# Turning q, the exponentials and the normalised rows by DMA instead of on TensorE in batches 2 to 4

## The chip, the cores and the metric

One core of one Trainium2 chip runs the whole program. The metric is the time of one execution on the device in microseconds (us); the median of several runs counts. The engines are TensorE (PE, with its weight loads as PEld), VectorE (DVE), ScalarE (ACT), GpSimd (POOL) and SyncE (SP). POOL and SP issue the transfers.

## The reference

Four batches, eight heads, 768 tokens, head size 64. Per head an 8x8 matrix P is normalised five times over rows and columns (Sinkhorn) and mixes the eight blocks of 96 keys and values. Each block of 96 queries then attends to its own mixed block of 96 keys. The result, 768 x 512 per batch, goes through a two-dimensional Fourier transform (the real part is added to it), a layer normalisation and an MLP of 512 to 2048 to 512.

```python
k_sorted = np.einsum('bhij,bhjcd->bhicd', P, k_b)
v_sorted = np.einsum('bhij,bhjcd->bhicd', P, v_b)
scores = scale * np.matmul(q_b, k_sb.transpose(0, 1, 2, 4, 3))
attn = np.exp(scores - np.max(scores, axis=-1, keepdims=True))
attn = attn / (np.sum(attn, axis=-1, keepdims=True) + 1e-09)
x = np.matmul(attn, v_sb)                  # heads side by side: 768 x 512
u = x + np.real(np.fft.fft(np.fft.fft(x, axis=1), axis=2))
un = (u - mu) / np.sqrt(var + 1e-06)
out = u + np.maximum(un @ w_ch1, 0.0) @ w_ch2
```

## The kernel before

Work is cut into steps, and a planner (`Plan`) orders them once, when the program is built. Each step has for each engine that may run it a cost in nanoseconds; a transfer has also a size (`kb`, in a model of DMA bandwidth) or a landing time (`hop`). The planner walks through a modelled time, gives each engine the step that could start first, and among steps within 40 ns the one of highest priority: earlier batches first, MLP products (`prio` from 1e6) last, so that they fill what attention leaves free on PE. Buffers come from rings of a few tiles (`ring`), the eight PSUM banks among them. The order that results is fixed; on the chip each engine takes its instructions in that order and waits on semaphores. SP's and POOL's queues of transfers are ordered in the same way.

One batch goes through these stages.

- *Loads.* `load_kq` (L408, POOL) loads k and q of a pair of heads as float16 with six tokens on one partition; `load_v` (L400, SP) loads v as float32.
- *Mix.* `q_mix`: PE turns q of a pair in twelve transposes (L592), and an ACT or DVE copy (L381 or L385) makes qT, 128 x 768. `k_mix`: PE multiplies k by the matrix of P (L609), and two copies (L383 or L387) write kz, which has the keys of a head on 64 of 128 partitions. `v_mix` (L563, L565) and `v_move` (L575, twelve transfers a batch) make vs, the mixed values with the key position on partitions.
- *Attention,* in halves of four blocks. `maxima`: four products qT by kz (L661) put queries on partitions, and DVE takes the row maxima (L664). `scores`: four products (L676) write minus the maximum into a bank, broadcast along the keys' partitions, and four more (L680) add kz by qT, so that the scores stand transposed, keys on partitions; one ACT exponential follows (L685). `minus_one` (L695 ACT or L697 DVE) subtracts 1 and writes eT. `values`: four products of eT by vs (L708), where row 96 of eT is all ones, then DVE's reciprocal and product (L713, L714) into xr.
- *Post.* Folding and the DFT over the sequence (L752, L764), the DFT over the model size (L797, L801), the residual (L828, L830), sums on POOL (L845, L846), a store of u to DRAM (L852, SP), statistics (L863), normalisation (L880), and `transpose_u`: four PE transposes of each tile of rows (L896) and a copy to unT.
- *MLP,* in two groups a batch: 64 products L924, ReLU on ACT (L930), 48 products L945, the sum with u (L952), which is loaded again by SP (L910), and an indirect store by POOL (L967).

Attention of the next batch runs beside post and MLP of those before it. Rings that matter here: `sm` (4 tiles of exponentials), `mxs` (6), eT (3, one a head), banks (8), unT (2).

Of the kernel before, what the change touches and what calls it, by code (L numbers as in the profile page):

```python
# [9 lines left out]
F32 = mybir.dt.float32  # L10
F16 = mybir.dt.float16
# [16 lines left out]
XSC = 64.0  # L28
RSC = 1.0 / XSC

PERM = np.array([6 * (p % 16) + p // 16 for p in range(BLK)])

# [270 lines left out]
def kernel(  # L305
# [60 lines left out]
    ring("mh", 1, [128, 2, 2 * LT], F16)  # L366
    plan.rings["eT"] = Ring([const.tile([97, NB, BLK], F16, name=f"eT{i}") for i in range(3)])
    eTs = plan.rings["eT"].tiles
# [35 lines left out]
    def load_kq(b, hp, need):  # L404
        hs = slice(2 * hp, 2 * hp + 2)
        for d, src, tag in ((k16, k, "k16"), (q16, q, "q16")):
            d[b, hp] = Buf(tag)
            step("load_" + tag, b, {"G": 740}, lambda e, t=d[b, hp], src=src: nc.gpsimd.dma_start(  # L408
                t.t, src[b, hs].rearrange("h (p g) d -> p h (g d)", g=G)),
                w=[d[b, hp]], kb=393, need=need)  # L410

# [38 lines left out]
    selj = const.tile([64, 128], F32, name="selj_sb")  # L450
    junk = const.tile([128, DM], F16, name="junk")
    nc.vector.memset(junk, 1.0)
# [36 lines left out]
    rsel = const.tile([BLK + 3, 2, BLK + 1], F16, name="rsel_sb")  # L489
    lm = const.tile([128, 2, 2, 385], F16, name="lm_sb")  # L490

# [91 lines left out]
    def q_mix(b, hp):  # L583
        qT[b, hp] = Buf("qT")
        pQ = Buf("bank")

# [8 lines left out]
        def ev(e):  # L595
            copy(e, qT[b, hp].t.rearrange("x (i g c) -> x i g c", g=G, c=16),
                 bank(pQ, [128, G, 128], F16).rearrange("x g (i c) -> x i g c", c=16))
        plan.chain(("psQ", b, {"T": 530}, f, [q16[b, hp]], [pQ]),
                   ("qT", b, {"A": 799, "V": 545}, ev, [pQ], [qT[b, hp]]))

    def k_mix(b, hp, gh):
# [11 lines left out]
        def ev(e, hh):  # L613
            r = slice(64 * hh, 64 * hh + 64)
            dst = kzs[hp][r, hh].rearrange("x (i g c) -> x i g c", g=G, c=16)
            copy(e, dst[:, :, 3 * gh:3 * gh + 3, :],
                 bank(pK, [128, 3, 128])[r].rearrange("x g (c i) -> x i g c", c=16), SCALE)
        plan.chain(("psK", b, {"T": 360}, f, [k16[b, hp], (kron[b], hp // 2)], [pK]),
# [48 lines left out]
    def scores(n, half):  # L667
# [5 lines left out]
        def f(e):  # L673
# [4 lines left out]
            for j in range(4):  # L678
# [7 lines left out]
                sms[n, half].t, bank(pS, [BLK, 4, BLK]), AF.Exp), [pS], [sms[n, half]]))  # L686

    def minus_one(n, half):
        if half == 0:
# [10 lines left out]
    def values(n, half):  # L700
# [3 lines left out]
        def f(e):  # L704
            ps = bank(pN, [BLK, 4, D + 1])
            for j in range(4):
                i = 4 * half + j
                nc.tensor.matmul(ps[:, j, :], eT[n].t[:, i, :],  # L708
                                 vs[2 * (b % 2) + h // 4][:, i, (D + 1) * (h % 4):(D + 1) * (h % 4 + 1)])
# [175 lines left out]
    def transpose_u(b, i, m):  # L885
# [3 lines left out]
        if (b, t // 4) not in unT:  # L889
            unT[b, t // 4] = Buf("unT")  # L890
        pY = Buf("bank")

# [130 lines left out]
    for hp in range(4):  # L1023
# [6 lines left out]
    warm(banks[7], 2)  # L1030
    ptm = plan.rings["sm"].tiles[3].rearrange("p a c -> p (a c)")[0:64, 0:256].rearrange(
        "p (i n) -> p i n", n=32)
# [63 lines left out]
    for b in range(B):  # L1096
# [63 lines left out]
```

## Time and profile before

| | |
|---|---|
| median of three runs | 347.85 us (345.82 to 349.72) |
| profiled execution | 349.94 us, span 348.2 us |
| PE busy | 316.3 us (91%) |
| DVE, ACT, POOL busy | 222.1, 212.3, 136.9 us |
| mean granted PE clock | 0.969 |
| DMA | 41.28 MB, 119 GB/s; q0 26.0% and q1 24.7% of 16 engines |
| chain that ended last, by engine | PE 62%, DVE 13%, issue 7%, DMA 7%, POOL 5%, ACT 4% |
| attention's products L676, L680, L661, L708 | 23.1, 22.9, 20.1, 19.5 us busy, 256 each |
| MLP's products L924, L945 | 89.0 us (512), 89.5 us (384) |

Matmuls overlap, and a busy time counts each of them from start to modelled end; what a run of matmuls really takes is read from the pace at which they start, in the timeline or the chain. The chain follows, from the last instruction backwards, what released each step. A stretch of the run is best judged by the busy times in that stretch, as the share over the whole span mixes stages of different kinds.

### The profile page before, as it was taken

The page shows a single profiled execution, that of the slowest core. Times are in us where ns is not written, and L with a number is a line of the kernel's source. Part 1 is how long each engine was busy: PE and PEld are TensorE (multiplying, and loading weights), DVE is VectorE, ACT ScalarE, POOL GpSimd, SP SyncE. Part 2 cuts the span into 40 slices and gives each one's busy share as a digit, 9 for nine tenths or more (in the row PEclk, how much of TensorE's full clock was granted, in tenths as well). Part 3 has the DMA queues.
Part 4 walks back from the last instruction along what each step waited for, and adds up shares of the span by engine and source line. Part 5 has one row for each costly group of instructions (what it writes and reads, how often), then busy time and mean ns, then how long its engine had stood idle before and what let it go on. Part 6 is the DMA issues. An engine that isn't in the chain of part 4 may idle for free.

```text
span 348.2 us, 8075 instructions
## 1 busy us (share of the span) xinstructions
PE 316.3 (91%) x3042; PEld 206.4 (59%) x3042; DVE 222.1 (64%) x577; ACT 212.3 (61%) x474; POOL 136.9 (39%) x190
## 2 busy tenths in 40 slices
PE   0998987867998999999989999999999999999994
PEld 0368854755766655678747867656556455554541
DVE  6688995996787799399989989983550602101001
ACT  5598885885787455788986846617537354260620
POOL 8879340175460599932100116651351420112111
PEclk9998998995799999999999999999999999999999
DMA  7999959079669397793530122243070330403212
GB/s 180 217 255 263 143 93 197 10 157 194 165 145 144 85 262 218 119 140 72 91 64 2 63 62 71 84 152 105 25 217 34 107 119 2 151 32 99 81 47 76
DMA packets 34799, 41.28 MB, mean 119 GB/s; under 512 B 4465, under 2 KB 26448, under 8 KB 34760
## 3 DMA queue, kind: packets, MB, share of 16 engines
q0 software_dynamic: 14992, 16.97, 26.0%
q1 hardware_dynamic: 19768, 23.80, 24.7%
q8 instruction: 24, 0.39, 0.5%
q14 instruction: 15, 0.12, 0.1%
HBM read 35.36 MB, written 12.58 MB: 138 GB/s over the span
## 4 chain that ended last, share of the span: by engine, by line
PE 62%; DVE 13%; issue 7%; DMA 7%; POOL 5%; ACT 4%; SPq 1%; POOLq 0%; DVEq 0%; ACTq 0%
PE bank L924 21%; PE bank L945 20%; DMA u_dram<-u 3%; DMA xr<-xr 3%; PE bank L676 3%; PE bank L680 2%; PE bank L708 2%; ACT kz L383 2%; PE bank L511 2%; DVE xr L714 2%; DVE mxs L664 2%; PE bank L592 1%; PE bank L661 1%; PE bank L801 1%; PE bank L752 1%
## 5 line engine op out<-in xcount | busy, mean ns | idle before, releaser
L930 ACT ACTIVATE hr<-bank 128x384 f16<-128x384 f32 x128 | 62.2, 490 | 59.3 <-PE bank L924 58.8
L945 PE MATMUL bank<-w2sb,hr 128*128 128x512 f16 x384 | 89.5, 379 | 0.0
L924 PE MATMUL bank<-unT,w1sb 128*128 128x384 f16 x512 | 89.0, 329 | 0.3 <-DVE unT L385 0.3
L924 PEld LDWEIGHTS <-w1sb 128*128 128x128 f16 x512 | 49.6, 99 | 32.5 <-issue 1.1
L967 POOL DMA_INDIRECT out_dram<-outt,idx_sb x23 | 22.7, 988 | 101.5 <-DVE outt L952 48.6
L945 PEld LDWEIGHTS <-hr 128*128 128x128 f16 x384 | 36.1, 98 | 37.9
L952 DVE SCALAR_TENSOR_TENSOR outt<-ur,bank 128x512 f32<-128x512 f32 x24 | 16.4, 683 | 49.1 <-PE bank L945 49.1
L880 DVE TENSOR_SCALAR un<-u,mv,rstd 96x512 f16<-96x512 f32 (+1 forms) x32 | 21.5, 703 | 33.4 <-PE bank L896 32.5
L685 ACT ACTIVATE sm<-bank 96x384 f32<-96x384 f32 x64 | 28.6, 484 | 8.3 <-PE bank L680 5.0
L664 DVE TENSOR_REDUCE mxs<-bank 96x4 f16<-96x384 f32 x64 | 31.6, 542 | 0.3
L714 DVE TENSOR_TENSOR xr<-bank,rz 96x256 f16<-96x256 f32 x64 | 26.9, 421 | 2.2
L845 POOL TENSOR_TENSOR u<-u,P 96x257 f32<-96x257 f32 (+1 forms) x16 | 11.9, 743 | 35.9 <-ACT u L381 21.5
L676 PE MATMUL bank<-nident_sb,mxs 96*96 96x96 f16 x256 | 23.1, 215 | 3.1 <-ACT u L381 2.0
L863 DVE BATCH_NORM_STATS2 st<-u 96x6 f32<-96x512 f32 (+1 forms) x32 | 21.8, 680 | 1.9 <-POOL u L846 1.9
L661 PE MATMUL bank<-kz,qT 128*96 128x96 f16 x256 | 20.1, 212 | 3.1 <-ACT kz L383 1.8
L680 PE MATMUL bank<-qT,kz 128*96 128x96 f16 x256 | 22.9, 214 | 0.0
L695 ACT ACTIVATE eT<-sm 96x384 f16<-96x384 f32 x46 | 22.7, 520 | 0.3 <-PE bank L708 0.2
L383 ACT ACTIVATE kz<-bank 64x384 f16<-64x384 f32 x45 | 21.3, 485 | 1.8 <-DVE kz L387 1.3
L676 PEld LDWEIGHTS <-mxs 96*96 96x96 f16 x256 | 18.9, 130 | 5.4 <-issue 2.9
L381 ACT COPY u<-bank 96x512 f32<-96x512 f32 (+1 forms) x26 | 14.5, 582 | 11.2 <-PE bank L830 4.5
L427 POOL TENSOR_TENSOR v<-v 128x384 f32<-128x384 f32 x11 | 11.7, 1066 | 22.6 <-ACT v L381 17.9
L708 PE MATMUL bank<-vs,eT 97*96 97x65 f16 x256 | 19.5, 213 | 0.9 <-DVE kz L387 0.4
(119 smaller groups left out, 549.7 us busy)
## 6 DMA issues: line engine op xcount, KB each, us to landing
u_dram<-u SPq DMA_DIRECT2D x32, 192.0 KB
ur<-u_dram SPq DMA_DIRECT2D x24, 256.0 KB
v<-in_v_dram SPq DMA_DIRECT2D x11, 384.0 KB
k<-in_k_dram POOLq DMA_DIRECT2D x16, 192.0 KB, 4.6
q<-in_q_dram POOLq DMA_DIRECT2D x16, 192.0 KB, 5.8
vs<-vo SPq DMA_DIRECT2D x42, 65.0 KB
w1sb<-in_moe_w_ch_dram POOLq DMA_DIRECT2D x4, 512.0 KB, 10.7
w2sb<-in_moe_w_ch_dram POOLq DMA_DIRECT2D x4, 512.0 KB, 8.2
```

Of the source, the lines that this page charges most:

```text
L383: nc.scalar.activation(dst, src, AF.Copy, scale=scale)
L661: nc.tensor.matmul(ps[:, j, :], qT[b, hp].t[:, col], kzs[hp][:, hh, col])
L664: ("max", b, {"V": 548}, lambda e: nc.vector.tensor_reduce(mxs[n, half].t, bank(pS, [BLK, 4, BLK]), axis=AX.X, op=ALU.max), [pS], [mxs[n, ...
L676: nc.tensor.matmul(ps[:, j, :], mxs[n, half].t[:, j:j + 1].broadcast_to([BLK, BLK]), nident, start=(j == 0), stop=False, skip_group_check= ...
L680: nc.tensor.matmul(ps[:, j, :], kzs[hp][:, hh, col], qT[b, hp].t[:, col], start=False, stop=True, skip_group_check=True)
L685: ("exp", b, {"A": 487}, lambda e: nc.scalar.activation(sms[n, half].t, bank(pS, [BLK, 4, BLK]), AF.Exp), [pS], [sms[n, half]]))
L695: nc.scalar.add(dst, sms[n, half].t, -1.0)
L708: nc.tensor.matmul(ps[:, j, :], eT[n].t[:, i, :], vs[2 * (b % 2) + h // 4][:, i, (D + 1) * (h % 4):(D + 1) * (h % 4 + 1)])
L714: nc.vector.tensor_tensor(xr2[b % 2][0:BLK, 4 * half:4 * half + 4, D * h:D * (h + 1)], ps[:, :, 0:D], rz.t[:, :, None].broadcast_to([BLK, ...
L924: nc.tensor.matmul(ps, w1sb[:, mc, 128 * fc:128 * fc + 128], unT[b, gr].t[:, mc, :], start=(mc == 0), stop=(mc == 3))
L930: nc.scalar.activation(dst, bank(pH, [128, 384]), AF.Relu)
L945: nc.tensor.matmul(ps, hr[f4].t[:, fc % 4, 128 * t:128 * (t + 1)], w2sb[:, fc, :], start=(fc == 0), stop=(fc == 15))
```

## The change

In the first batch nothing changes but the order of the queries in a block, which becomes the natural one (`PERM`, with the tables made from it), and ring sizes. In the second to fourth batch:

- q is loaded with another layout, token g*128+p on partition p, in two transfers a pair (rows of 64 elements, for six times 64 before). SP issues a DMA transpose of the q tile, which writes qT; the PE transposes and the copy go.
- kz gets the opposite sign. Scores are multiplied once a half, queries on partitions; DVE takes the minimum (of the negated scores) from that bank, and ACT makes the exponential from the same bank with the minimum as its bias: four activations of 96x96 a half, as each block has a bias of its own, for one of 96x384.
- The subtraction of 1 writes a float16 tile es, padded to 128 columns a block with ones (set once), and SP issues a DMA transpose of es into the half of eT that `values` reads. The ones arrive in rows 96 to 127.
- Of the eight tiles of normalised rows of a batch, seven are turned by DMA transposes issued by SP; the eighth, of 97 rows, stays on PE.
- The planner gets costs for these: 1200 ns of SP for each turn and 2500 ns until it has landed, 1080 ns for the four exponentials, 1600 ns of POOL and a size of 600 in the place of 393 for a q load.
- To make room, `sm` has three tiles for four, `mxs` four for six (first batch only), rings `mns` and `es` have three each, eT has 128 partitions for 97, and the tile for warming up PE shares memory with a table.

```diff
+QKB = 600
-PERM = np.array([6 * (p % 16) + p // 16 for p in range(BLK)])
+PERM = np.arange(BLK)
...
-    ring("mxs", 6, [BLK, 4], F16)
-    ring("sm", 4, [BLK, 4, BLK], F32)
+    ring("mxs", 4, [BLK, 4], F16)
+    ring("mns", 3, [BLK, 4], F32)
+    ring("es", 3, [BLK, 4, 128], F16)
+    ring("sm", 3, [BLK, 4, BLK], F32)
...
+                tq = t.t.rearrange("p a x -> p (a x)").rearrange("p (g h d) -> p g h d", g=G, h=2)
+                for hh in range(2):
+                    nc.gpsimd.dma_start(tq[:, :, hh], src[b, 2 * hp + hh].rearrange(
+                        "(g p) d -> p g d", g=G))
+            step("load_" + tag, b, {"G": 740 if b == 0 or tag == "k16" else 1600}, f,
+                 w=[d[b, hp]], kb=393 if b == 0 or tag == "k16" else QKB, need=need)
...
     def q_mix(b, hp):
         qT[b, hp] = Buf("qT")
+        if b:
+            step("turn_q", b, {"S": 1200}, lambda e: nc.sync.dma_start(
+                qT[b, hp].t.rearrange("x (g p) -> x g p", g=G),
+                q16[b, hp].t.rearrange("p a x -> p (a x)"), transpose=True),
+                r=[q16[b, hp]], w=[qT[b, hp]], hop=2500)
+            return
...
+    def turned(n, half):
...
+        def f(e):
+            ps = bank(pS, [BLK, 4, BLK])
+            for j in range(4):
+                col = slice(BLK * (4 * half + j), BLK * (4 * half + j + 1))
+                nc.tensor.matmul(ps[:, j, :], qT[b, hp].t[:, col], kzs[hp][:, hh, col])
+        def x(e):
+            for j in range(4):
+                nc.scalar.activation(sm.t[:, j, :], bank(pS, [BLK, 4, BLK])[:, j, :], AF.Exp,
+                                     bias=mn.t[:, j:j + 1], scale=-1.0)
...
+        plan.chain(
+            ("psS", b, {"T": 185}, f, [qT[b, hp]] + [("kz", hp, hh, g_) for g_ in range(2)], [pS]),
+            ("max", b, {"V": 548}, lambda e: nc.vector.tensor_reduce(
+                mn.t, bank(pS, [BLK, 4, BLK]), axis=AX.X, op=ALU.min), [pS], [mn]),
+            ("exp", b, {"A": 1080}, x, [pS, mn], [sm]))
+        step("minus", b, {"V": 459, "A": 518}, g, r=[sm], w=[es])
+        step("turn_e", b, {"S": 1200}, lambda e: nc.sync.dma_start(
+            et.t[:, 4 * half:4 * half + 4, :], es.t.rearrange("q j k -> q (j k)"), transpose=True),
+            r=[es], w=[(et, half)], hop=2500)
...
+        if b and (i, m) != (0, 1):
+            step("turn_u", b, {"S": 1200}, lambda e: nc.sync.dma_start(
+                unT[b, t // 4].t[:, :, BLK * (t % 4):BLK * (t % 4) + BLK],
+                un[b, i, m].t[0:BLK], transpose=True),
+                r=[un[b, i, m]], w=[(unT[b, t // 4], t % 4)], hop=2500)
+            return
...
+    for t in plan.rings["es"].tiles:
+        nc.gpsimd.memset(t[:, :, BLK:128], 1.0)
...
             for half in range(2):
+                if b:
+                    turned(n, half)
+                    continue
                 maxima(n, half)
                 scores(n, half)
                 minus_one(n, half)
```

More of the change, by code (lines that the diff above doesn't have):

```diff
@@ L366 @@
     ring("mh", 1, [128, 2, 2 * LT], F16)
-    plan.rings["eT"] = Ring([const.tile([97, NB, BLK], F16, name=f"eT{i}") for i in range(3)])
+    plan.rings["eT"] = Ring([const.tile([128, NB, BLK], F16, name=f"eT{i}") for i in range(3)])
     eTs = plan.rings["eT"].tiles
@@ L595, in ev @@
         def ev(e):
-            copy(e, qT[b, hp].t.rearrange("x (i g c) -> x i g c", g=G, c=16),
-                 bank(pQ, [128, G, 128], F16).rearrange("x g (i c) -> x i g c", c=16))
+            copy(e, qT[b, hp].t.rearrange("x (p g) -> x p g", g=G),
+                 bank(pQ, [128, G, 128], F16).rearrange("x g p -> x p g"))
         plan.chain(("psQ", b, {"T": 530}, f, [q16[b, hp]], [pQ]),
```

28 lines of the change are left out of this document (20 added, 8 removed).

## Prediction

> **What bounds the kernel now.** I read the slices of the page first, then the busy times by stretch, the chain that ended last, the groups of instructions by shape, and last the timeline and the DMA landings where the change cuts in.
>
> Busy times by stretch (us from:to, length, then busy time and count of each engine, granted clock, DMA share, GB/s):
>
> ```profile
> 60.00:80.00 20.00, 16.24 (x268) 14.07 (x269) 18.39 (x44) 16.67 (x39) 7.99 (x12) 0.93 0.48 92
> 80.00:100.00 20.00, 17.42 (x156) 12.87 (x155) 14.15 (x44) 13.69 (x34) 9.87 (x15) 0.72 0.79 185
> ...
> 160.00:180.00 20.00, 18.42 (x264) 13.62 (x263) 17.67 (x58) 18.33 (x43) 2.46 (x3) 1.00 0.47 96
> 180.00:200.00 20.00, 19.08 (x302) 15.56 (x300) 18.59 (x53) 15.26 (x37) 1.02 (x1) 1.00 0.09 29
> 200.00:220.00 20.00, 20.00 (x163) 13.34 (x162) 17.94 (x55) 11.03 (x27) 6.70 (x9) 1.00 0.23 68
> 220.00:240.00 20.00, 19.95 (x138) 11.88 (x136) 16.52 (x37) 9.77 (x26) 12.26 (x15) 1.00 0.46 138
> ```
>
> From 200 us PE is full. Up to 100 us no single engine is: PE, DVE and ACT take turns. The chain in its last third is PE alone, the two MLP products:
>
> ```profile
> 258.22 10.40 PE bank L924 x64
> 268.62 0.86 PE bank L945 x4
> 269.48 0.35 PE bank L896 x8
> ...
> 280.11 10.40 PE bank L924 x64
> ```
>
> So a group of the MLP costs 10.4 us for 64 L924 and 12 x 0.86 us for 48 L945, 20.8 us; eight groups are 166. The first L924 starts at 86.2 us. From there PE always has MLP work to take while attention waits, provided the written order puts it there; from there to the end of the products PE idles some 7 us (1.8 to 100 us, 5.0 from 100 to 200). PE time removed after 86 us is therefore time saved, PE time removed before it is not.
>
> **The change part by part.** Pace is read where PE runs without a gap, since a busy mean (215 ns for L676) counts overlap.
>
> ```profile
> 162.45 0.26 PEld L676 LDWEIGHTS <-mxs 96*96 96x96 f16 x4
> 162.63 0.26 PEld L680 LDWEIGHTS <-kz 128*96 128x96 f16 x4
> 162.81 0.30 PEld L676 LDWEIGHTS <-mxs 96*96 96x96 f16 x4
> ```
>
> In the chain, twelve q transposes in a row:
>
> ```profile
> 168.89 0.46 PE bank L592 x12
> ```
>
> *Second score product (L676, L680) gone in 48 halves:* 0.36 us from one half to the next (162.45 to 162.81), 17.3 us. *q transposes (L592) gone for 12 pairs:* twelve a pair in 0.46 us, 5.5 us. *Transposes of normalised rows (L896) gone for 21 of 32 tiles:* eight in 0.34 to 0.35 us, 0.17 a tile, 3.6 us. Together 26.4 us of PE. Before 86 us lie 12 of batch 1's 16 halves (48 of its 64 L676 stand in 60 to 80 us) and its four q pairs: 4.3 + 1.8 = 6.1 us, counted as nothing. That leaves **20.3 us** saved.
>
> *ACT.* One exponential of 96x384 (484 ns) becomes four of 96x96. Between 204 ns for 96x2 (L874) and 484 ns for 96x384 lie 0.73 ns an element, so 273 ns each, 1.09 us a half, 0.61 more; 48 halves add 29 us. The row with a bias (L873, 293 ns for 96x2) would make it 362 ns each and 46 us. Copies saved: about nine qT (804 ns) and 14 unT (477 ns), 14 us. ACT goes from 212 to 227 us (ends 212 and 245), below PE either way. The cover is MLP on PE; without it, 0.6 us a half over 48 halves, 29 us, would be exposed. I take 0. DVE loses a few copies and keeps its maximum at 542 ns; 0.
>
> *The turn of the exponentials: a new wait.* PE's L708 now waits for SP's issue and a transfer. The planner reserves 1.2 us for issue plus 2.5 us, 3.7. Behind a late L708 stand all later products, MLP too, as PE takes them in order. The trace has no such transfer. The nearest are SBUF to SBUF:
>
> ```profile
> 174.67 0.55 SPq L553
> ...
> 175.26 2.45 DMA xr<-xr
> ...
> DMA to landing us min/median/max: 4.5/5.0/5.8
> ```
>
> The first is at a DMA share of 0.47: 3.04 us from issue. The last line is vs<-vo from POOL near 22 us, when DMA is saturated. The ends are 3.04 and 5.8 us. Three es tiles let three halves be in flight, so PE loses an excess once per three halves. In batch 1, during loads of weights and u (share 0.5 to 0.8), I take 5.0: 1.3 too late; the first six halves are hidden because L708 of that batch waits for vs anyway, which leaves ten halves, 3.3 rounds, **4.3 us**. In batches 2 and 3 the share was 0.09 to 0.47 for most of the time, the 3.04 us row is nearest: nothing late in 10.7 rounds. The built order also covers: between the first and last L708 of batches 2 and 3 PE's queue holds 128 L924 and 96 L945 (41 us), where the kernel before had 0 and 40.
>
> A rule of the Trainium skill speaks against this part: VectorE: DVE Perf Modes, section The three transpose paths and its rules, prefers TensorE for a 128x128 transpose when PSUM will do and gives 1309 ns to the crossbar against 390. The measured TensorE pace here, 0.46 us for twelve 128x64, is far below its 390 ns. By the Trainium skill's crossbar figure a half (three such squares) would take 3.9 us and, on top of issue, be about 1.4 us late in every round, an estimated 20 us, which would leave no gain. No transfer in this trace shows it.
>
> *SP and its queue.* 81 turns of 1.2 us are 97 us of SP in about 250. They stand in one queue with u stores, ur loads and v loads; in the built order batch 2's four v loads come behind 16 turns of batch 1. SP already waits in ur loads, which would then hold a turn back:
>
> ```profile
> SPq L910 <- DVE outt L952: 76.9, 16, 14.1
> SPq L852 <- POOL u L846: 59.1, 25, 14.4
> ```
>
> Most of these lie in the last third, with no exponential behind them; 0, with the first rival as the other end.
>
> *q loads.* Twelve loads become two issues each: 12 x 0.74 = 8.9 us of POOL. Rows shrink from 1536 to 256 bytes, 1536 rows for 256. At equal time a byte nothing is added; at equal time a row (97 ns: 26% of 16 x 348 us over 14992 packets) 80 rows an engine add 7.7 us a load. POOL carries the chain around 89 to 117 us. I take **2.0 us** (ends 0 and 31, the four loads of batch 1). *u turns* replace L896 and a copy; in the built order three MLP groups (62 us) stand behind the last post; 0. *First batch:* three memsets before POOL's loads (0.32 us for twice the size) and a smaller sm ring: **1.0 us** (ends 0 and 3).
>
> Sum: -20.3 + 4.3 + 2.0 + 1.0 = -13.0 us. The profiled execution took 349.94 (span 348.2 and 1.7 around it), 2.1 above the median 347.85 of the three runs. On the median: **335 us**.
>
> **Rivals.**
>
> *Turns late everywhere (slower).* Place: L708 of all three batches, 14 exposed rounds. It decides where 14 rounds eat 20.3 - 3.0 = 17.3 us: 1.24 late each, landing 4.9 us after issue. At the 5.8 us end: 14 x 2.1 = 29 us, -20.3 + 3.0 + 29.4 = +12.1, **360 us**. For it: 5.0 us landings of vs<-vo, stores of 192 KB of 3.70 and 8.10 us at 72 and 76 us, 12 times the bytes of the 2.45 us row. At 8.10 + 1.2 us it would be 409. Against: DMA was little used from 160 us on.
>
> *Turns follow one another in one stream (slower, far).* Units of 96 KB: 48 e, 21 u, 12 q of two, 93. From about 60 us to 285 us (last post must leave three groups) they fit if one takes under 2.4 us. At half the 8.10 us store, 4.05 each: 60 + 93 x 4.05 + 41.6 = about **478 us**. Half the 3.70 us store, 1.85, fits. The Trainium skill's 1309 ns a square (VectorE: DVE Perf Modes) would be 3.9 us a unit, were squares not to overlap; its DMA: Bandwidth & Descriptors, Latency and other measured facts, has 261 GB/s for transposes instead, 0.4 us a unit.
>
> *The gain is eaten (no change).* DVE and ACT bind batches 1 to 3 rather than PE: at 160 to 200 us they are 36.3 and 33.6 of 40 us busy beside PE's 37.5; ACT's net 14 us then come back as PE idle, beside the 7.3 us of the other terms: -20.3 + 21.3 = +1.0, **349 us**. Against: the built order gives PE 41 us of MLP there.
>
> *PE's own idle shrinks too.* More MLP among the attention also fills the 7 us idle after 86 us, and no added term shows: 347.85 - 20.3 - 7 = **321 us**.
>
> **How the numbers follow.** Forecast 335 us: 0.42, own range 325 to 344. 321 us: 0.10. Eaten, 349 us: 0.10. Late turns, 352 to 409 with 360 as its price: 0.32, nearly all over 1%. One stream, 478: 0.06. 1% either way is about what a measurement of this kernel can tell from no change. Faster 0.52, same 0.10, slower 0.38. The range reaches from 318 to 378 us: it leaves out the stream rival, a tenth for the tail of late turns, and little below.
>
> **What would show it.** Right: L676 down to 64 and L592 to 48; PE busy about 290 us; PE in front of L708 waiting for eT's transfer under 10 us in all; turns landing 3 to 4 us after issue from 140 us on; the last attention interleaved with L924. Wrong: tens of us of PE idle ended by the transfer of eT or qT, SP busy in the turns well over 1.2 us each, or first L924 much later than 86 us, which would put the fault in the first batch or the loads. A full PE and still no gain would refute the pace of the removed products.

## The result and the profile after

The changed kernel takes 358.36 us (median of 4 runs, 355.94 to 359.55) against 348.11 us (345.82 to 349.72) for the kernel before in the same session: ratio 1.0291, interval 1.0209 to 1.0373. It is 2.9% slower; the forecast was 335 us. The profiled execution took 359.55 us, its span is 357.8 us and the mean granted TensorE clock 0.916.

First the busy times by stretch of the changed kernel, the same stretches and columns as shown of the kernel before, and then its total busy times from the page:

```profile
60.00:80.00 20.00, 10.54 (x96) 6.98 (x95) 17.91 (x43) 12.41 (x44) 6.49 (x9) 0.89 0.54 101
80.00:100.00 20.00, 8.79 (x70) 6.89 (x70) 11.15 (x23) 7.27 (x26) 9.38 (x13) 0.50 0.98 180
...
160.00:180.00 20.00, 15.92 (x129) 8.96 (x125) 12.84 (x28) 13.43 (x48) 11.32 (x15) 0.95 1.30 175
180.00:200.00 20.00, 16.61 (x160) 11.74 (x160) 13.49 (x47) 14.24 (x41) 1.38 (x2) 0.79 0.68 148
200.00:220.00 20.00, 19.29 (x164) 11.51 (x165) 18.49 (x43) 15.38 (x50) 10.15 (x13) 1.00 0.79 145
220.00:240.00 20.00, 16.31 (x164) 11.86 (x162) 16.44 (x42) 12.93 (x40) 6.47 (x9) 0.99 0.53 134
```

```profile
PE 297.7 (83%) x2430; PEld 185.1 (52%) x2430; DVE 238.3 (67%) x606; ACT 205.7 (57%) x556; POOL 148.3 (41%) x204
```

PE lost the work that it was to lose: 612 fewer instructions, and 18.6 us less busy time (316.3 before). That is less than the 26.4 us of the prediction; the largest part of the rest is in the 512 MLP products L980 (L924 before), which are busy for 96.3 us in place of 89.0, some of them at a lower granted clock (0.50 from 104 to 108 us, 0.79 in the mean from 180 to 200). But span minus busy time, PE's idle time, went from 31.9 to 60.1 us, 28.2 more. The difference, 9.6 us, is the longer span. The idle time grew in every part of the attention: by 14.3 us from 60 to 100 us (19.33 of 40 us busy, 33.66 before), by 8.2 us from 100 to 200, by 4.4 us from 200 to 260. DVE, which was to lose a few copies, has 16.2 us more to do.

The chain in order of time in the changed kernel shows the worst of the waits (start, length, what):

```profile
82.00 1.46 PE bank L758 x16
...
85.21 9.59 DMA eT<-es
94.80 0.02 issue
94.83 0.35 DVE es L727
95.18 0.10 DVE rz L763
...
95.31 0.43 DVE xr L764
...
95.78 0.48 PE bank L952 x4
...
105.21 0.71 PE bank L980 x3
105.92 7.14 DMA eT<-es
...
113.14 0.04 ACT es L725
...
160.10 1.03 ACT sm L719 x4
...
161.78 4.82 DMA eT<-es
...
259.50 3.45 DMA eT<-es
...
289.95 10.07 PE bank L980 x62
```

A turn issued at 85.21 us is released 9.59 us later; one at 161.78 us after 4.82, and one at 259.50 us, right behind a load of u, after 3.45. These are landings on the chain. By the packets and semaphores of the trace the mean is 5.0 us for the 16 turns of the second batch and 3.2 us for 28 of the 32 later ones (the semaphore records of the other four are not complete), and a turn with nothing ahead of it takes 2.3. What waits for the first is not PE in front of the value product, as the prediction had it, but DVE, which cannot write the next `es` tile until the turn has read it. All that stands behind on DVE (L763, L764, a copy) comes 6.9 us late, and PE starts its transposes of the first batch's normalised rows (L952), which wait for L764, only at 95.78. The first MLP product starts at 105.0 us (86.2 before). At the end of the run the price of an MLP product is what it was, 10.07 us for 62 where 64 took 10.40, and the four exponentials of a half follow one another in 1.03 us. The landing is only the last part of the time for which that `es` tile is held. Two lines of SP's queue in the second batch, with no turn between them (start, length):

```profile
74.11 1.29 SPq L734 DMA_TRANSPOSE eT<-es  x1
...
85.21 3.15 SPq L734 DMA_TRANSPOSE eT<-es  x2
```

The turn at 85.21 us is the seventh of its batch, and its `es` tile had been written by 71.1 us (the seventh writing in the trace), 14.1 us before the issue. eT has three tiles of two halves, so six turns find a free one; the seventh needs the tile of the first head, which the value product L758 reads only at 82.00 us, in the first line of the chain above. In the next two batches the tile of the seventh turn lies for 13.3 and 9.2 us in the same way, and the turn is issued within 2 us of the first L758 of its batch (182.4 and 229.1 us).

The waits of the changed kernel, all engines (total us, times, longest):

```profile
POOL q L417 <- DMA qT<-q: 36.0, 2, 19.2
...
ACT sm L719 <- DVE mns L730: 12.6, 10, 3.4
...
ACT es L725 <- DMA eT<-es: 11.5, 7, 3.1
...
DVE es L727 <- DMA eT<-es: 7.4, 2, 6.9
PEld L758 <- DMA vs<-vo: 7.4, 2, 5.6
...
PE bank L952 <- DVE xr L764: 6.9, 1, 6.9
...
PEld L758 <- DMA eT<-es: 2.2, 5, 1.0
```

ACT and DVE wait 18.9 us for the three `es` tiles, PE only 2.2 us in its weight loads and 0.6 us in its products for eT itself. SP's own issues are as reserved (instances, ns minimum/median/maximum), and its longest waits are shorter than before, 47.2 and 22.2 us where they were 76.9 and 59.1:

```profile
L734 SPq DMA_TRANSPOSE eT<-es x48: 1179/1207/2315, 56.7 to 260.9; - x48
```

```profile
SPq L966 <- DVE outt L1008: 47.2, 12, 13.5
SPq L902 <- POOL u L896: 22.2, 16, 9.0
```

GpSimd (first line) stands still for 36.0 us, in two pieces, at loads of q whose tile still waits for its turn, and its sums of u and v stand behind them; what that costs, no run shows by itself.

Read this far, the turns that land late in the second batch look like the whole cause. That theory was the first to be tried, and as the whole cause it did not hold.

### The profile page after: what moved, and what is told of

Read it like the earlier page. It is cut to its first block, busy times and chain, and to the rows that moved or that the text cites. A ratio compares the mean times of both kernels' runs of the same rounds, so it can differ in the third digit from the quotient of the medians.

```text
span 357.8 us, 7109 instructions
## 1 busy us (share of the span) xinstructions
PE 297.7 (83%) x2430; PEld 185.1 (52%) x2430; DVE 238.3 (67%) x606; ACT 205.7 (57%) x556; POOL 148.3 (41%) x204
## 4 chain that ended last, share of the span: by engine, by line
PE 50%; DMA 17%; DVE 15%; ACT 6%; issue 5%; POOL 3%; SPq 1%; POOLq 0%; DVEq 0%; ACTq 0%
PE bank L980 17%; PE bank L1001 16%; DMA eT<-es 10%; PE bank L758 3%; ACT sm L719 2%; DMA out_dram<-outt,idx_sb 2%; PE bank L521 2%; ACT kz L386 2%; PE bank L802 2%; DVE xr L764 2%; POOL u L896 1%; DMA unT<-un 1%; POOL u L895 1%; DMA qT<-q 1%; DVE mns L730 1%
## 5 line engine op out<-in xcount | busy, mean ns | idle before, releaser
L980 PE MATMUL bank<-unT,w1sb 128*128 128x384 f16 x512 | 96.3, 339 | 4.2 <-DVE u L388 1.9
L1001 PE MATMUL bank<-w2sb,hr 128*128 128x512 f16 x384 | 89.3, 379 | 0.0
L980 PEld LDWEIGHTS <-w1sb 128*128 128x128 f16 x512 | 50.2, 102 | 37.4 <-issue 9.4
L1001 PEld LDWEIGHTS <-hr 128*128 128x128 f16 x384 | 36.3, 98 | 39.0 <-issue 0.8
L719 ACT ACTIVATE sm<-bank,mns 96x96 f32<-96x96 f32 x192 | 47.6, 342 | 13.1 <-DVE mns L730 12.6
L417 POOL DMA_DIRECT2D q<-in_q_dram x24 | 20.0, 846 | 36.5 <-DMA qT<-q 36.0
L758 PE MATMUL bank<-vs,eT 97*96 97x65 f16 x256 | 21.6, 225 | 8.6 <-DMA ur<-u_dram 5.2
L764 DVE TENSOR_TENSOR xr<-bank,rz 96x256 f16<-96x256 f32 x64 | 26.9, 421 | 2.2
L758 PEld LDWEIGHTS <-eT 97*96 97x96 f16 x256 | 20.0, 145 | 14.5 <-DMA vs<-vo 7.4
L730 DVE TENSOR_REDUCE mns<-bank 96x4 f32<-96x384 f32 x48 | 25.2, 543 | 0.2 <-PE bank L715 0.2
L727 DVE TENSOR_SCALAR es<-sm 96x384 f16<-96x384 f32 x23 | 11.4, 514 | 14.4 <-DMA eT<-es 7.4
L725 ACT ACTIVATE es<-sm 96x384 f16<-96x384 f32 x25 | 12.9, 526 | 11.8 <-DMA eT<-es 11.5
L715 PE MATMUL bank<-kz,qT 128*96 128x96 f16 x192 | 15.3, 215 | 5.0 <-DVE amt L543 1.0
L715 PEld LDWEIGHTS <-qT 128*96 128x96 f16 x192 | 14.3, 131 | 9.3 <-issue 4.8
L384 ACT CAST W<-bank 128x384 f16<-128x384 f32 (+1 forms) x33 | 14.0, 437 | 5.4 <-DVE W L388 2.2
```

The source lines that it names most:

```text
L715: nc.tensor.matmul(ps[:, j, :], qT[b, hp].t[:, col], kzs[hp][:, hh, col])
L719: nc.scalar.activation(sm.t[:, j, :], bank(pS, [BLK, 4, BLK])[:, j, :], AF.Exp, bias=mn.t[:, j:j + 1], scale=-1.0)
L730: ("max", b, {"V": 548}, lambda e: nc.vector.tensor_reduce(mn.t, bank(pS, [BLK, 4, BLK]), axis=AX.X, op=ALU.min), [pS], [mn]),
L758: nc.tensor.matmul(ps[:, j, :], eT[n].t[0:97, i, :], vs[2 * (b % 2) + h // 4][:, i, (D + 1) * (h % 4):(D + 1) * (h % 4 + 1)])
L764: nc.vector.tensor_tensor(xr2[b % 2][0:BLK, 4 * half:4 * half + 4, D * h:D * (h + 1)], ps[:, :, 0:D], rz.t[:, :, None].broadcast_to([BLK, ...
L980: nc.tensor.matmul(ps, w1sb[:, mc, 128 * fc:128 * fc + 128], unT[b, gr].t[:, mc, :], start=(mc == 0), stop=(mc == 3))
```

## The experiments

Every expectation was written before its run. The kernel before ran beside each set, with medians of 346.48 to 348.63 us; each ratio is to the runs beside it. "Second batch" is batch index 1, the first in which the change acts.

**The parts alone.** The turns of the normalised rows (u), of q, and of the exponentials (e), each with the other two parts undone; u and q alone with the ring sizes of the kernel before.

```diff
-        if b and (i, m) != (0, 1):          # u     (and alike for q_mix and turned)
+        if b >= 9 and (i, m) != (0, 1):
```

u alone: 

> Only the normalised rows are turned by DMA; q and the exponentials go through TensorE as before, rings at their old sizes. Theory 1 (the turns of the exponentials in batch 1 land late, in the stretch with weight loads and u traffic, and hold es tiles, so that DVE and ACT stand and the first MLP product starts at 105 us): no such turns here, first MLP product at 86 to 90 us, 3.6 us less PE, 342 to 348 us. Theory 2 (SyncE's queue is full of issues of 1.2 us): 21 more issues, mostly in post, 345 to 352 us.

q alone: 

> Only q is loaded in small rows and turned by DMA; exponentials and normalised rows as before, rings at their old sizes. Theory 1: no turn of exponentials, first MLP product at 86 to 92 us, 5.5 us less PE of which 3.7 count, 342 to 348 us. Theory 3 (the 1536 small rows of each q load take the DMA engines from the loads that the first batches need): most of the loss is here, first MLP product after 95 us and 352 us or more.

e alone: 

> Only the exponentials are turned by DMA, with the score product done once; q and normalised rows through TensorE as before. Theory 1: most of the loss is here, first MLP product at 98 to 106 us, writers of es wait for the turn 10 us or more, 350 to 358 us. Theory 3: the loss is gone, first MLP product by 90 us, 335 to 342 us.

All parts from the third batch on (b >= 2): 

> All three turns in the third and fourth batch only; the second batch as before the change (with the smaller rings). Theory 1 and theory 2 alike (the trouble is the second batch, amid weight loads, u traffic and moves of v): first MLP product at 86 to 92 us, PE 17.6 us less, 335 to 345 us. If turns are late everywhere: 348 us or more.

The same without q's turns: 

> Exponentials and normalised rows turned in the third and fourth batch only; q loaded and turned as before in all batches. If the small rows of the q loads (DMA share over 1 from 140 to 180 us with all three turns in these batches) hold back the third batch: idle of PE from 140 to 180 us falls from 9 to under 4 us and the time is 338 to 344 us. If it is the turns of the exponentials themselves: 346 to 352 us.

Measured: u alone 350.12 us, ratio 1.0061 (1.0017 to 1.0104); q alone 348.74 us, 1.0037 (0.9988 to 1.0086); e alone 371.04 us, 1.0749 (1.0643 to 1.0854); all parts from the third batch on 347.75 us (342.63 to 348.33) against 347.39, no difference that can be told; so leaving the second batch as it was takes back the loss, but brings no gain. e and u from the third batch on 357.71 us, 1.0256 (1.019 to 1.0322). e alone and e with u lie above everything that was expected of them. Nothing adds: u and q take PE work away for no gain, e alone costs 23.7 us, yet with q and u it costs 10, and from the third batch on q's turns make the kernel 10 us *faster*. Parts that change sign with what stands beside them point away from a price of each and towards something that all of them change.

**The late landings of the second batch.** Three ways to relieve them in the changed kernel. Few weights: a quarter of the MLP's weights is loaded and used four times (not the reference's MLP). Stores by POOL: the u stores leave SP's queue. Four es tiles: a small table moved to make room.

```diff
-    for i in range(8):
+    for i in (0, 4):
         weights(i,
```
```diff
-        step("store_u", b, {"S": 350}, lambda e: nc.sync.dma_start(
+        step("store_u", b, {"G": 760}, lambda e: nc.gpsimd.dma_start(
```
```diff
-    ring("es", 3, [BLK, 4, 128], F16)
+    ring("es", 4, [BLK, 4, 128], F16)
```

> The changed kernel with only the first of four pieces of each MLP weight loaded (2 of 8 MB; the products use that piece four times over, so the MLP is not the reference's). Theory 1a (in batch 2 the turns land late because they share the DMA engines with the weight loads): first MLP product at 88 to 95 us instead of 105, waits for es under 8 us instead of 18.9. Theory 1b (they stand behind u stores and u loads in the same queue): first MLP product still after 98 us.

> The changed kernel with the stores of u issued by GpSimd, so that they leave SyncE's queue. Theory 1b: first MLP product at 88 to 96 us, turns of batch 2 land in under 6 us, 345 to 353 us. Theory 1a: no change, first MLP product after 98 us, 355 to 360 us.

> The changed kernel with four es tiles instead of three (a table of the start shares memory to make room). Theory 1 (late turns stop DVE and ACT through the es ring): waits for es fall by a third or more, first MLP product 3 to 8 us earlier, 350 to 356 us. If PE's wait for eT is what counts: no change, 356 to 360 us.

Measured: 356.89 us (ratio 1.0306, 1.024 to 1.0372), 362.21 us (1.0459, 1.0389 to 1.053) and 362.2 us (357.26 to 367.14). None gains. Two of them did move what they were to move, the first MLP product, from 105 us to 87.6 (few weights) and 89.4 (four tiles). The waits of the writers of `es` for a turn were to fall from 18.9 us to under 8 with few weights, and fell to 13.5; with four tiles they rose, to 27.9. Busy times by stretch with few weights:

```profile
80.00:100.00 20.00, 13.04 (x95) 8.66 (x94) 13.59 (x33) 11.23 (x38) 9.34 (x13) 0.59 1.09 205
100.00:120.00 20.00, 16.86 (x134) 11.32 (x134) 14.81 (x50) 13.91 (x35) 11.50 (x16) 0.79 1.15 167
120.00:140.00 20.00, 16.09 (x153) 10.42 (x152) 17.54 (x40) 16.42 (x50) 6.60 (x10) 0.83 0.82 137
...
200.00:220.00 20.00, 15.42 (x144) 10.29 (x143) 15.21 (x41) 14.54 (x51) 9.61 (x13) 1.00 0.63 166
```

PE gains 4.3 us at 80 to 100 us and gives back 3.9 at 120 to 140 (20.00 in the changed kernel) and 3.9 at 200 to 220. The late start of the MLP is not what sets the end: what does not wait there waits later. The landings themselves were relieved only in part, and each of the three edits also leads the planner to another order, so these runs speak against the late landings as the sole cause, but do not price them. Why a fourth `es` tile does not help, the trace shows: the seventh to tenth writings of each batch then lie for 12 to 17 us before their turns are issued, as it is eT that is not free.

**Ceilings.** What is left of the change if the turn of the exponentials costs nothing? In the first run the value product reads the unturned `es`; in the second one exponential with one bias replaces the four, and the planner is told 487 ns for it; in the third q is not turned either.

```diff
-        step("turn_e", b, {"S": 1200}, ...)          # run 1; values() reads es
-            for j in range(4): nc.scalar.activation(sm.t[:, j, :], ..., bias=mn.t[:, j:j + 1], scale=-1.0)
+            nc.scalar.activation(sm.t, bank(pS, [BLK, 4, BLK]), AF.Exp, bias=mn.t[:, 0:1], scale=-1.0)   # run 2
-            ("exp", b, {"A": 1080}, x, [pS, mn], [sm]))
+            ("exp", b, {"A": 487}, x, [pS, mn], [sm]))
-            step("turn_q", b, {"S": 1200}, ...)       # run 3
+            qT[b, hp] = q16[b, hp]
```

> The turn of the exponentials is left out in the second to fourth batch: the value product reads the unturned exponentials themselves, without the row of ones (so these are not the reference's values), with the same dependency on the writer and the same 48 single score products. Theory L (the turn's landing, 6 to 9 us where 3.7 were reserved, is the loss): the gain that was forecast appears, 333 to 342 us. Theory B (the removed TensorE time is worth nothing in these stretches, because VectorE and ScalarE set the attention's pace): 347 to 352, like the kernel before. Theory A (four exponentials in place of one make the chain longer): 350 to 358.

> As the run without the turn, and one exponential over the four columns with one bias in place of four (also not the reference's values). Theory A: at least 6 us below the run without the turn alone. Theories L and B: within 3 us of it.

> The run with one exponential and no turn of the exponentials, and in the second to fourth batch the score product reads the unturned q as well: neither TensorE nor a DMA turns it, with five q tiles in place of three and two qT in place of four (scores and values are not the reference's). If removed TensorE time is saved where no turn lands late, the 20 us appear: 324 to 331 us. If the missing 8 us never were a saving (TensorE waits in the attention for VectorE and ScalarE whatever it has to do), 333 to 338 us.

Measured: 344.11 us (ratio 0.9891, 0.9814 to 0.9967), 335.26 us (0.964, 0.9585 to 0.9696), 343.18 us (0.9858, 0.979 to 0.9927). So the turn of the exponentials, with all that the planner then orders in another way, is worth 14.3 us between the changed kernel and the first run, and the shorter exponential with its lower told cost 8.9 us more. The third run is the surprise: it leaves out still more work than the second and is 7.9 us slower, against both expectations. Its work is a part of the other's, and PE has as many instructions (2430); what differs is their order, which is computed anew, and the number of q tiles and qT tiles.

**What the planner is told.** Four runs change the told costs and the exponentials apart from each other. On the kernel before: four exponentials of 96 columns and a told 1080 ns; then the told 1080 ns alone.

```diff
-            ("exp", b, {"A": 487}, lambda e: nc.scalar.activation(
+            ("exp", b, {"A": 1080 if b else 487}, lambda e: nc.scalar.activation(
```

> The kernel before, with each exponential of batches two to four written as four of 96 columns, nothing else. 96 halves' worth of 48 get 0.6 us more of ScalarE each, 29 us in all. Theory A: 355 to 365 us. Theories L and B: within 4 us of the kernel before.

> The kernel before, its one exponential per half unchanged, but its planner told 1080 ns for it in batches two to four in place of 487; only the order differs. Theory O (the 14 us of four exponentials came from the order written for the told cost): 355 to 365 us. Theory A (they came from the four instructions themselves): within 4 us of the kernel before.

(In the first of these texts it is 48 halves that get 0.6 us more each, and its "nothing else" does not hold: the planner is told 1080 ns too.) Measured: 361.58 us (ratio 1.0393, 1.0334 to 1.0453) with four exponentials, 361.78 us (1.0437, 1.0362 to 1.0511) with the told cost alone. The number told to the planner costs 14.9 us; the four instructions on top of it cost nothing. In the trace of the first, the four are little longer than the one: 192 take 29.5 us of ACT, 0.61 a half, where the one took 0.48. The groups of ACT in that run (count, busy, mean ns):

```profile
L685 ACT ACTIVATE sm<-bank 96x96 f32<-96x96 f32 x192 | 29.5, 273 | 10.2 <-PE bank L680 9.9
L685 ACT ACTIVATE sm<-bank 96x384 f32<-96x384 f32 x16 | 7.0, 480 | 1.5 <-PE bank L680 1.1 <-ACT sm L685 0.3
```

What the told cost does is seen in the groups of DVE, first the kernel before, then the kernel before with 1080 ns told, then the changed kernel:

```profile
L697 DVE TENSOR_SCALAR eT<-sm 96x384 f16<-96x384 f32 x18 | 6.7, 384 | 0.9 <-PE bank L708 0.6 <-ACT sm L685 0.2
...
L385 DVE COPY u<-bank 96x512 f32<-96x512 f32 x6 | 4.1, 681 | 3.4 <-PE bank L830 2.8 <-PE bank L828 0.6
...
L385 DVE CAST vo<-bank 128x384 f16<-128x384 f32 x4 | 2.0, 552 | 0.0
```

```profile
L697 DVE TENSOR_SCALAR eT<-sm 96x384 f16<-96x384 f32 x41 | 14.9, 386 | 0.5 <-PE bank L708 0.5
```

```profile
L388 DVE COPY u<-bank 96x512 f32<-96x512 f32 (+1 forms) x17 | 11.4, 683 | 5.5 <-PE bank L880 3.6 <-DMA u_dram<-u 1.3 <-PE bank L878 0.5
L727 DVE TENSOR_SCALAR es<-sm 96x384 f16<-96x384 f32 x23 | 11.4, 514 | 14.4 <-DMA eT<-es 7.4 <-issue 2.9 <-ACT hr L986 2.1
L388 DVE CAST vo<-bank 128x384 f16<-128x384 f32 x19 | 9.6, 546 | 0.0
```

Copies and the subtraction of 1 may run on ACT or DVE. Told that ACT will be busy for 1.08 us a half, the planner gives them to DVE: with the told cost alone 41 of 64 subtractions in place of 18; in the changed kernel 19 copies of vo in place of 4 and 17 of u in place of 6, beside 23 of the 48 subtractions of its new path. DVE's busy time goes from 222.1 to 231.6 us with the told cost and to 238.3 in the changed kernel. In one stretch DVE has no room for it. Busy times by stretch, one line of the kernel before (its other lines stand in the prediction), then the kernel before with 1080 ns told:

```profile
140.00:160.00 20.00, 19.66 (x279) 14.71 (x278) 14.01 (x31) 15.41 (x38) 11.09 (x17) 1.00 0.78 113
```

```profile
60.00:80.00 20.00, 13.86 (x224) 11.29 (x222) 18.34 (x43) 12.77 (x31) 7.81 (x11) 0.92 0.40 95
80.00:100.00 20.00, 14.47 (x164) 12.20 (x164) 14.52 (x38) 9.66 (x23) 11.15 (x16) 0.74 0.72 174
...
140.00:160.00 20.00, 17.59 (x299) 14.82 (x297) 19.30 (x51) 13.81 (x32) 11.63 (x17) 1.00 0.71 127
160.00:180.00 20.00, 16.52 (x216) 11.71 (x216) 18.91 (x57) 15.39 (x34) 1.41 (x2) 0.98 0.34 63
```

From 140 to 180 us DVE is busy for 38.2 of 40 us (31.7 before), ACT for 29.2 (33.7 before), and PE loses 4.0 us. That is not the whole of the 14.9: at 60 to 100 us PE loses 5.3 more, and there DVE is as busy as before (32.9 us for 32.5) and ACT less (22.4 for 30.4). So the price of the told number is measured; that the copies on DVE are its cause is a reading for a part of it, as no run moves the copies alone, and none tells the kernel before another number.

On the changed kernel: one exponential in place of four under the unchanged order; the told landing of the turns raised; and as a control one told cost raised by 2%.

```diff
-            for j in range(4): nc.scalar.activation(sm.t[:, j, :], ..., bias=mn.t[:, j:j + 1], scale=-1.0)
+            nc.scalar.activation(sm.t, bank(pS, [BLK, 4, BLK]), AF.Exp, bias=mn.t[:, 0:1], scale=-1.0)
```
```diff
-            r=[es], w=[(et, half)], hop=2500)
+            r=[es], w=[(et, half)], hop=7000 if b == 1 else 3500)
```
```diff
-            ("max", b, {"V": 548}, lambda e: nc.vector.tensor_reduce(
+            ("max", b, {"V": 560}, lambda e: nc.vector.tensor_reduce(
```

> The changed kernel with its order and told costs unchanged, but one exponential per half with the first block's maximum as the bias of all four (a wrong maximum for three of the four blocks, which the division by the row sum takes out again). ScalarE is done about 0.5 us sooner in each of 48 halves. Theory A: 347 to 351 us. Theory O: 355 to 360, as the changed kernel.

> The changed kernel, its planner told that a turn of the exponentials lands 7.0 us after its issue in the second batch and 3.5 us in the later ones, in place of 2.5; only the order written differs. Theory L: an order that allows for the landing takes back half of the loss, 346 to 352 us. Theories A and B: 355 to 362, as the changed kernel.

> The changed kernel, its planner told 560 ns for each maximum of batches two to four in place of 548; nothing else. If what an order is worth is a matter of what it is written for (the landing of the turns), this gives 355 to 361 us, as the changed kernel. If any other order moves the time by as much as the seven and more microseconds seen with a longer landing, it lies outside 353 to 363, and the gain of the longer landing is then no proof of its cause.

Measured: 361.61 us (ratio 1.0414, 1.0336 to 1.0492), 349.56 us (1.0003, 0.9956 to 1.0049) and 361.2 us (1.0445, 1.0361 to 1.0529). Under the unchanged order, ACT's shorter work (186.5 us busy for 205.7) gains nothing: it waits for the `es` tiles instead, 27.3 us for all writers of `es` where it was 18.9. Told the longer landing, the same work takes 8.8 us less, and the ratio's interval lies wholly below that of the changed kernel. Of the 11.0 us by which the two profiled spans differ, 4.7 are PE idle and 6.3 PE busy (291.4 for 297.7, at a mean granted clock of 0.955 for 0.916), and DVE has no less to do than before, 241.2 us for 238.3. The control moved by 2.8 us (by the ratios 1.5%, some 5 us), to 0.2 us above the upper end of what was expected, so a gain of 8.8 is more than that one other order made; one control is no distribution, though, and the third ceiling shows that 7.9 us can also come unbidden. With the longer landing PE waits *more* for eT (13.3 us in its products); the writers of `es` wait less, 9.5 us for 18.9. The instructions on `es` in that run: what they waited for, then who waited for them, the turn among them (total us, times):

```profile
  DMA eT<-es: 9.5, 8
...
  PEld L758: 14.9, 6
  PE bank L758: 13.3, 4
  DVE es L727: 6.6, 5
  ACT es L725: 2.9, 3
```

**A version that both findings point to.** One maximum over a query's four blocks as the bias of one exponential (the bias divides out of the softmax, so any common one serves; told 560 ns), with the longer told landing: in all three batches, and in the third and fourth alone.

```diff
-                mn.t, bank(pS, [BLK, 4, BLK]), axis=AX.X, op=ALU.min), [pS], [mn]),
+                mn.t, bank(pS, [BLK, 4 * BLK]), axis=AX.X, op=ALU.min), [pS], [mn]),
-            for j in range(4): nc.scalar.activation(sm.t[:, j, :], ..., bias=mn.t[:, j:j + 1], scale=-1.0)
+            nc.scalar.activation(sm.t, bank(pS, [BLK, 4, BLK]), AF.Exp, bias=mn.t, scale=-1.0)
```

> The changed kernel with one maximum over a query's four blocks as the bias of one exponential (told 560 ns), and the planner told the longer landing of the turns (7.0 us in the second batch, 3.5 us later). If the prices add, 349.6 less 9: 338 to 343 us, below the kernel before. If the order is a matter of luck, anything from 340 to 355.

> Every edit in the third and fourth batch alone, with one maximum over a query's four blocks as the bias of one exponential (told 560 ns) and a landing of 3.5 us told for the turns of the exponentials. If the second batch, with no product of the MLP beside it, holds what the longer landing did not take back, 335 to 343 us. If the turns cost as much in the later batches, 345 to 350 us.

Measured: 348.24 us in all three batches (ratio 1.0025, 0.9986 to 1.0064), against the expectation: the two prices do not add. DVE has 16.3 us less to do there than with the longer landing alone (224.9 for 241.2), and the time is the same (1.0025 for 1.0003): DVE's load, too, does not set the time by itself. In the third and fourth batch alone 339.62 us (4 runs, 336.24 to 341.91; the kernel before beside it 348.63, 7 runs, 345.63 to 349.32; the two do not overlap, and the medians stand as 0.974, for which there is no interval). It is faster than both kernels. Its busy times from the page, and by stretch:

```profile
PE 298.3 (89%) x2634; PEld 189.9 (57%) x2634; DVE 226.9 (68%) x584; ACT 198.9 (59%) x445; POOL 144.4 (43%) x201
```

```profile
80.00:100.00 20.00, 18.52 (x199) 14.24 (x198) 17.12 (x51) 14.26 (x33) 11.46 (x17) 0.90 0.71 164
...
160.00:180.00 20.00, 16.55 (x180) 11.30 (x179) 15.23 (x44) 15.08 (x35) 4.33 (x6) 1.00 1.32 163
...
200.00:220.00 20.00, 16.38 (x138) 10.30 (x139) 17.97 (x46) 14.21 (x36) 12.26 (x17) 1.00 0.67 170
```

PE is 18.0 us less busy than in the kernel before, nearly as in the changed kernel, but idles 37.7 us (span 336.0), only 5.8 more. The stretch at 80 to 100 us, with the second batch done in the old way, is whole again, and DVE has 226.9 us, 4.8 more than before. Some of the price stays: PE has 3.5 us idle at 160 to 180 and 3.6 at 200 to 220.

The runs side by side (PE idle is the span less PE's busy time; MLP is the start of the first MLP product):

| kernel | median us | ratio | PE busy | PE idle | DVE busy | MLP at |
|---|---|---|---|---|---|---|
| before | 348.11 | | 316.3 | 31.9 | 222.1 | 86.2 |
| changed | 358.36 | 1.0291 | 297.7 | 60.1 | 238.3 | 105.0 |
| before, 1080 ns told | 361.78 | 1.0437 | 320.3 | 39.4 | 231.6 | 92.2 |
| changed, one exponential, same order | 361.61 | 1.0414 | 294.2 | 67.1 | 241.5 | 106.6 |
| changed, maximum told 560 ns | 361.2 | 1.0445 | 296.8 | 60.4 | 235.9 | 103.6 |
| changed, longer landing told | 349.56 | 1.0003 | 291.4 | 55.4 | 241.2 | 97.4 |
| no turn of e | 344.11 | 0.9891 | 297.0 | 44.4 | 232.7 | 94.2 |
| no turn of e, one exponential | 335.26 | 0.964 | 295.9 | 37.1 | 224.5 | 92.7 |
| the same, no turn of q | 343.18 | 0.9858 | 299.7 | 41.3 | 220.3 | 81.0 |
| one bias, longer landing, batches 2 to 4 | 348.24 | 1.0025 | 292.1 | 55.6 | 224.9 | 94.2 |
| one bias, longer landing, batches 3 and 4 | 339.62 | | 298.3 | 37.7 | 226.9 | 84.3 |

In the kernels with the change in all three batches PE is busy for 291.4 to 299.7 us; what differs most is its idle time. DVE's busy time does not order the times: 241.2 us stand beside 349.56, and 235.9 beside 361.2.

## Why the prediction was wrong

Step by step, in the order of the prediction.

- *"PE time removed after 86 us is therefore time saved" (-20.3 us): the step that failed.* The work went, and idle time came in its place: PE busy fell by 18.6 us and PE idle rose by 28.2, from 31.9 to 60.1. The step rests on "PE always has MLP work to take while attention waits", and that needs the MLP's inputs: these come through DVE and ACT, which stand in the same fixed orders behind the waits of the attention (6.9 us at once for a free `es` tile on DVE and on PE behind it). The best that a run without a late turn shows is 12.5 us (335.26 against 347.75), and a like run shows 5.5 (343.18 against 348.63). Whether 20 us can be had under another order is not settled.
- *"The written order":* the prediction took the order as cover and asked only whether MLP products stand in PE's queue behind a wait. They did stand there (in the trace 116 L980 and 64 L1001 between the first and the last L758 of its batches 2 and 3). It did not ask which engine the planner gives the copies to, nor that the planner recomputes all of it from the told costs. That has a measured price in the kernel before, 14.9 us for a told 1080 ns. How much of it falls to the changed kernel is not shown: 8.9 us separate the two ceilings, in which the told cost and the operation change together, the operation alone gained nothing under the changed kernel's order, and one exponential told at 560 ns gained nothing beside the longer landing (1.0025 for 1.0003).
- *"DVE loses a few copies ... 0":* false by 16.2 us of busy time. The built order, which the prediction read for PE, has DVE's instructions as well.
- *ACT, 0:* right as to the instructions. Four exponentials with a bias take 342 ns each (273 taken, 362 the end), and follow one another at 1.03 us a half; under the unchanged order one exponential in their place gains nothing (361.61 us).
- *The turn of the exponentials, 4.3 us:* mis-sized. Leaving it out saves 14.3 us, in another order. The landings were taken rightly in the mean, 5.0 us in the second batch and 3.04 later (measured 5.0 and 3.2), though the two in the second batch that stand in the chain took 9.59 and 7.14. Wrong was what they were charged to. "Three es tiles let three halves be in flight" counts a tile from its turn's issue; the trace has tiles that lie for up to 14.1 us before it, for want of a free eT. And PE hardly waits for eT; DVE and ACT wait for a free `es` tile and hold up what stands behind them.
- *SP and its queue, 0:* right as to SP's own time, 1.2 us an issue. But the v loads that the prediction saw behind the 16 turns of the second batch are issued at 122 to 150 us (31 to 86 before), and the first value product of the third batch starts at 182.4 us (155.5 before), of the fourth at 229.1 (188.4). What that costs is open: with the longer landing told, at 349.56 us, these products start as late (183.9 and 224.8). *q loads, 2.0 us, u turns, 0:* q alone gives 1.0037 and u alone 1.0061, so neither is dear, but neither gains what it takes from PE (5.5 and 3.6 us). *First batch, 1.0 us:* no run takes it by itself.
- *The rivals.* "Turns late everywhere", 360 us, has the time nearly right and the condition met in the second batch (its limit was 4.9 us). Its place, L758 on PE, is not where the time goes, and three reliefs of the second batch's landings did not bring it back; leaving that batch unchanged took the loss back, without the gain. "The gain is eaten" (349 us; 350 with the 15 us of ACT that the prediction's own sum gives for its 14) named DVE and ACT as the engines that would bind, and counted nothing more on DVE. With the turns' own price beside it, it is the nearer story as to the place, the waits of DVE and ACT; that their load is what binds is not shown.
- *What was to show it:* PE busy about 290 us came only in part (297.7); the short waits for eT in front of the value product came (2.8 us), and so did landings of 3 to 4 us or less from 140 us on for most of the turns. These were to show it right. The first MLP product "much later than 86 us" came too, and was to put the fault in the first batch or the loads; in the chain it lay in the waits for `es`.

What stays open: how the 14.3 us of the turn divide between the landings, the wait for a free eT before them, the queue of SP and the order written for them. The changed kernel and its two runs with other told numbers, which do the same work, differ by 11.6 us with the order (349.56 to 361.2), so no term from these runs is good to better than that.

## What to carry to other kernels

Where an order is computed from told costs, a change of one cost is a change of the whole program: compare, engine by engine, what each is given before and after, and whether an engine that feeds the bound (here DVE) got more; but do not take its load for the cause before a run has shown it. Work taken from the bounding engine is time saved only if what feeds it next comes no later; look for who waits for the *source* buffer of a new transfer, not only for its result, and for what the transfer itself must wait before it can be issued. And before pricing a term by leaving it out, run one control in which nothing but the order changes.

## What was not expected of the hardware

- A DMA transpose of a 96x512 half-precision tile (98 KB in 384 rows of 256 bytes) has, in the trace of the changed kernel, its first packet 1.2 us after the issue begins, its data within 0.64 us after that, and is released 2.3 us after the issue when nothing is ahead of it (the turns at 67.25, 157.91 and 230.88 us, among others); while weights, stores and other turns were under way, first packets came 4.1 to 6.1 us after the issue for five of the seven turns issued between 85 and 106 us, and one release 9.59 us after it. The data of the free case move at 154 GB/s (98,304 bytes in 0.64 us). The Trainium skill (VectorE: DVE Perf Modes, The three transpose paths) gives 1309 ns for a square of 128; three of them one after another would be 3.9 us, an estimate from that figure, and the whole turn took 2.3, so here they overlap or cost less. The Trainium skill's rule (the same page, Rules for kernel authors) that TensorE is to be preferred where PSUM will do agrees with the changed kernel, at 1.0291, but the last version keeps the turns in two batches and is faster than the kernel before, so the case does not settle it.
- The granted clock is 0.50 in the whole stretch from 80 to 100 us of the changed kernel, in which PE is busy for 8.79 of 20 us, and the work after an idle time pays again: the first four L980, at 105.02 us, span 1.47 us, four at 112.37 us span 0.81 (the granted clock is 1.00 from 110 us on). The Trainium skill (TensorE: Matmul & The Clock Gate, Part 1) has a gate that halves the clock after an idle window; the trace agrees.
- Four activations of 96 columns from PSUM take ACT 0.61 us a half, little more than the one of 384 (0.48), where there is no bias from a tile (the kernel before with four exponentials); with one they take 1.03 (the changed kernel).
